# Second and third token group: the second expert product in seven block products, from split weights kept in DRAM

## The chip, the cores and the metric

The kernel runs on one core of a Trainium2 chip. The metric is the device time of one execution in microseconds (us). A core has TensorE (PE: matrix products into the PSUM banks), VectorE (DVE), ScalarE (ACT) and GpSimd (POOL) for elementwise work, SyncE (SP), which here only issues transfers, and 16 DMA engines between DRAM and the on-chip SBUF.

## The reference

An attention layer makes the 2304 x 512 input `x` of a mixture of experts; only the second half matters here:

```python
N, D, E, F = (2304, 512, 8, 1024)
P = ...                       # 2304 x 8, eight rounds of row and column scaling
for e in range(E):
    h = np.maximum(x @ w1[e], 0.0)
    ye = h @ w2[e]
    out += P[:, e:e + 1] * ye
```

All of it is float32, and all P are positive.

## The kernel before

Every float32 operand of a matrix product is held as two rounded parts, a high one (`h` at the end of a name) and a low one (`l`), and a product is three: high by high, high by low, low by high. ACT makes the high part (a copy), POOL or DVE the low part (a subtraction).

The experts come behind attention, in `experts()`. The 2304 tokens are three groups of 768. The work on one group, for one expert and one quarter (256 columns) of its hidden layer, is an **item**; a group has 31 of them (the 32nd, of expert 0, is done for all tokens during attention), and the groups follow each other, so that all weights are loaded and split three times over. An item has two products:

- The first, `x @ w1`, is 2 x 2 blocks by 2 x 2 blocks. `first_fast` makes it in seven block products instead of eight (a scheme of Strassen's kind): POOL makes four sums of weight blocks (L979 to L984), and `t_tasks` four sums of token blocks once for a group; a block product is six matmuls of 128x384 (L1024). DVE adds the products to the four quarters of h (L1055); ACT takes relu and the high part (L1008), DVE the low part (L1009). The items in the set `plain` (four at the start, two at the end of the first and of the second group) use eight block products.
- The second, `h @ w2`, is `product2`: 36 matmuls of 128x512 (L838), six for each 128 tokens, with h as the weights. DVE multiplies each result by P and adds it to `acc` (L1095), which goes to `out` at the end of a group.

PE does the first product of item q, then the second product of item q - 1. Meanwhile POOL and ACT split the weights of the items that follow (L969 to L998). On ACT and DVE the order is as the code has it, on the others a scheduler sets it; every engine runs its instructions in order, and waits where a result or a buffer isn't there.

## Time and profile before

| | |
|---|---|
| median of 3 runs | 1727.99 us (1727.05 to 1728.17) |
| the profiled execution | 1727.62 us, of which the span from first to last instruction is 1725.8 us |
| busy share of the span | PE 99%, DVE 72%, POOL 67%, ACT 41% |
| granted clock of PE | 1.00 of full speed (2.4 GHz) |
| DMA | 135 MB, mean 78 GB/s |

A busy share says how long an engine had an instruction in work, not that it worked at its peak, and a mean over the span hides stages with different limits.

### The profile page before, as it was taken

How to read it: one execution, taken by the hardware profiler on the slowest of the kernel's cores; microseconds unless marked ns; L12 is line 12 of the kernel's file. 1: busy time of each engine (PE TensorE's matmuls, PEld its weight loads, DVE VectorE, ACT ScalarE, POOL GpSimd, SP SyncE). 2: the span in 40 equal slices, each digit the busy share in tenths (PEclk: the TensorE clock that was granted, in tenths of full speed). 3: DMA queues.
4: the chain of work that ended last, by engine and by line, in shares of the span. 5: the costliest groups of instructions: out<-in, count | busy, mean ns of one | idle time of the engine just before them, and what ended most of it. 6: DMA issues, size and time to landing. Idle time of an engine off the chain costs nothing.

```text
span 1725.8 us, 26878 instructions
## 1 busy us (share of the span) xinstructions
PE 1707.8 (99%) x9381; PEld 1519.2 (88%) x9381; DVE 1250.3 (72%) x2307; ACT 707.1 (41%) x1632; POOL 1148.6 (67%) x1091
## 2 busy tenths in 40 slices
PE   7999999999999999999999999999999999999999
PEld 6777879899989999899989998899899998999887
DVE  8877747877777777777777777777777777777776
ACT  7877743333333333343333333332343333333332
POOL 5755544576667766577677666775677667766673
PEclk9999999999999999999999999999999999999999
DMA  5444333222222222232222222212332222212221
GB/s 137 101 108 103 94 110 107 68 61 62 74 74 68 61 68 74 74 129 68 73 74 62 61 74 74 71 60 73 93 116 60 68 73 74 63 60 73 74 62 49
DMA packets 150215, 135.02 MB, mean 78 GB/s; under 512 B 68288, under 2 KB 116544, under 8 KB 150080
## 3 DMA queue, kind: packets, MB, share of 16 engines
q1 hardware_dynamic: 148304, 132.22, 26.1%
q8 instruction: 74, 1.21, 0.3%
q10 hardware_dynamic: 1776, 1.09, 0.2%
q14 instruction: 61, 0.50, 0.1%
HBM read 123.75 MB, written 9.51 MB: 77 GB/s over the span
## 4 chain that ended last, share of the span: by engine, by line
PE 97%; DVE 1%; DMA 1%; ACT 1%; POOL 0%; issue 0%; SPq 0%; POOLq 0%; ACTq 0%; DVEq 0%
PE s L838 44%; PE s L1024 30%; PE f L1024 10%; PE x L648 2%; PE s L408 2%; PE s L489 1%; PE f L838 1%; PE f L817 1%; PE s L313 1%; PE s L455 1%; PE x L653 1%; PE s L623 1%; PE s L715 0%; PE s L540 0%; PE s L508 0%; PE s L817 0%
## 5 line engine op out<-in xcount | busy, mean ns | idle before, releaser
L975 POOL TENSOR_TENSOR w1l<-raw,w1h 128x512 fp32r<-128x512 f32 x263 | 365.9, 1404 | 396.0 <-ACT w1h L974 387.7
L1095 DVE SCALAR_TENSOR_TENSOR acc<-s,P,acc 128x512 f32<-128x512 f32 x540 | 395.0, 744 | 146.7 <-PE s L838 146.7
L838 PE MATMUL s<-w2h,hhl 128*128 128x512 f32 x1116 | 436.1, 391 | 0.0
L838 PE MATMUL s<-w2l,hhh 128*128 128x512 f32 x1116 | 435.8, 391 | 0.0
L838 PE MATMUL s<-w2h,hhh 128*128 128x512 f32 x1116 | 434.8, 390 | 0.0
L1055 DVE TENSOR_TENSOR temps<-s,temps 128x384 f32<-128x384 f32 x447 | 242.3, 554 | 173.2 <-ACT w1h L974 86.5
L1009 DVE SCALAR_TENSOR_TENSOR hhl<-temps,hhh 128x384 fp32r<-128x384 f32 x340 | 304.8, 896 | 0.0
L998 POOL TENSOR_TENSOR w2l<-raw,w2h 128x512 fp32r<-128x512 f32 x186 | 292.8, 1594 | 10.5 <-ACT w2h L997 10.5
L1008 ACT ACTIVATE hhh<-temps 128x384 fp32r<-128x384 f32 x340 | 178.7, 526 | 295.3 <-DVE temps L1055 287.7
L838 PEld LDWEIGHTS s<-w2h,hhl 128*128 128x128 f32 x1116 | 209.4, 188 | 43.9
L838 PEld LDWEIGHTS s<-w2h,hhh 128*128 128x128 f32 x1116 | 209.6, 188 | 42.4 <-DVE acc L1095 1.1
L838 PEld LDWEIGHTS s<-w2l,hhh 128*128 128x128 f32 x1116 | 209.5, 188 | 41.6
L1058 ACT COPY temps<-s 128x384 f32<-128x384 f32 x64 | 30.7, 480 | 416.2 <-PE s L1024 409.4
L1024 PE MATMUL s<-th,w1h 128*128 128x384 f32 x510 | 170.3, 334 | 0.0
L1024 PE MATMUL s<-tl,w1h 128*128 128x384 f32 x510 | 170.3, 334 | 0.0
L1024 PE MATMUL s<-th,w1l 128*128 128x384 f32 x510 | 170.3, 334 | 0.0
L1024 PE MATMUL s<-xh,w1l 128*128 128x384 f32 x480 | 161.3, 336 | 0.4 <-POOL w1l L970 0.4
L1024 PE MATMUL s<-xh,w1h 128*128 128x384 f32 x480 | 161.4, 336 | 0.0
L1024 PE MATMUL s<-xl,w1h 128*128 128x384 f32 x480 | 160.8, 335 | 0.0
L974 ACT CAST w1h<-raw 128x512 fp32r<-128x512 f32 x263 | 154.2, 616 | 3.0 <-DMA raw<-in_moe_w_dram 3.0
L1055 DVE TENSOR_TENSOR temps<-f,temps 128x384 f32<-128x384 f32 x148 | 80.3, 554 | 57.5 <-ACT w1h L974 28.5
L997 ACT CAST w2h<-raw 128x512 fp32r<-128x512 f32 x186 | 111.9, 607 | 0.0
(216 smaller groups left out, 2841.1 us busy)
## 6 DMA issues: line engine op xcount, KB each, us to landing
raw<-in_moe_w_dram SPq DMA_DIRECT2D x372, 256.0 KB
rsb<-rd SPq DMA_DIRECT2D x32, 144.0 KB
ydr<-wst SPq DMA_DIRECT2D x18, 256.0 KB
acc<-ydr SPq DMA_DIRECT2D x18, 256.0 KB
qraw<-in_q_dram SPq DMA_DIRECT2D x32, 128.0 KB
vraw<-in_v_dram SPq DMA_DIRECT2D x32, 128.0 KB
kraw<-in_k_dram SPq DMA_DIRECT2D x30, 128.0 KB
out_dram<-acc SPq DMA_DIRECT2D x15, 256.0 KB
```

Of the source, the lines that this page charges most:

```text
L408: nc.tensor.matmul(out=sp[h][:, at:at + w], lhsT=qq[x][half[h], 128 * i:128 * i + 128], rhs=kk[y][half[h], 0:w], start=(a == 0), stop=(a = ...
L648: nc.tensor.matmul(out=x[half[h], a0:a1], lhsT=vs[:, kt, h], rhs=ee(h), start=(kt == 0), stop=False,)
L838: nc.tensor.matmul(out=pt, lhsT=h_[:, f, cols], rhs=w[:, f], start=(n == 0), stop=(n == 5))
L974: nc.scalar.copy(out=wh[:, i:i + 2], in_=src)
L975: tt(out=wl[:, i:i + 2], in0=src, in1=f32(wh[:, i:i + 2]), op=ALU.subtract)
L997: nc.scalar.copy(out=wh[:, j], in_=raws[j])
L998: nc.gpsimd.tensor_tensor(out=wl[:, j], in0=raws[j], in1=f32(wh[:, j]), op=ALU.subtract)
L1008: nc.scalar.activation(out=hh[:, f, c], in_=src, func=AF.Relu)
L1009: late.append(lambda: nc.vector.scalar_tensor_tensor(out=hl[:, f, c], in0=src, scalar=0.0, in1=f32(hh[:, f, c]), op0=ALU.max, op1=ALU.subt ...
L1024: nc.tensor.matmul(out=pt[:, 0:HT], lhsT=w[:, wi, k], rhs=x[:, k], start=(n == 0), stop=(n == total - 1),)
L1055: nc.vector.tensor_tensor(out=o, in0=x, in1=y, op=ALU.add)
L1095: nc.vector.scalar_tensor_tensor(out=acc[:, j], in0=pt, scalar=P[:, t_, e:e + 1], in1=acc[:, j], op0=ALU.mult, op1=ALU.add,)
```

## The change

The first group stays, and writes its split weights to DRAM on the way: `keep` the seven parts of w1 with their low parts into `cache`, `keep2` three of the four blocks of w2 into `cache3`; `w1_again` makes those of the four plain items at the start. P goes to DRAM transposed (`pd`).

The second and third group are written as a list of timed steps (`at`), sorted by time (with a table `SHIFT` of some 700 numbers added, and a table `ON` that says whether DVE or POOL takes an operation), and all engines run in this order. Items go in pairs: both first products (`fast`), then both second products (`sums`). The second product is now transposed, with w2 as the weights and h (already multiplied by P, `pb`) as the moving side, and is also made in seven block products, two row halves each, with three matmuls of 128x384 for every half: 42 for an item. The two items of a pair add up in PSUM, and DVE adds the banks to 14 blocks `macc` (tiles `m`); two of the seven products stay in PSUM for the next pair. For the seven products, DVE and POOL make four sums of blocks of h (`combos`) and their low parts, and in the second group four sums of blocks of w2, which `cache2` keeps for the third. At the end of a group `group_end` joins `macc` to four quarters, and `close` turns them back by PE transposes, adds the start values from `ydr` and writes `out`. The last pair of the second group uses eight block products for the first product (`slow`), while `t_again` makes the token sums of the third group.

```diff
         ITEMS = [
-            (g, e, part) for g in range(NG) for e in range(E) for part in range(NQ)
-            if (e, part) != (0, 0)
+            (0, e, part) for e in range(E) for part in range(NQ) if (e, part) != (0, 0)
         ]
...
-        scaled = [(0, 1, 0)] + [(g, 0, 1) for g in range(1, NG)]
-        plain = set(range(4)) | {g * per - j for g in range(1, NG) for j in (1, 2)}
+        scaled = [(0, 1, 0)]
+        plain = set(range(4)) | {per - 1, per - 2}
+        cache = dram.tile([per, 8, 128, 2, 256], F32, name="cache")
+        cache2 = dram.tile([per, 2, 128, 512], F32, name="cache2")
+        cache3 = dram.tile([per, 3, 128, 2, 256], F32, name="cache3")
...
+            def keep(q=q, ops=slice(0, 7), to=slice(0, 7)):
+                for i, w in enumerate((wh, wl)):
+                    nc.sync.dma_start(
+                        out=cache[q, to, :, i].rearrange("o p c -> p o c"),
+                        in_=f32(w[:, ops]).rearrange("p o k c -> p o (k c)"),
+                    )
...
+            return [lambda: two(1, r1), lambda: one(0, a11)] + rest
...
-            return [lambda: one(0), lambda: one(1)]
+            def keep2():
+                for i, w in enumerate((wh, wl)):
+                    w = f32(w)
+                    nc.sync.dma_start(out=cache3[q, 0, :, i], in_=w[:, 0, 0:256])
+                    nc.sync.dma_start(
+                        out=cache3[q, 1:3, :, i].rearrange("o p c -> p o c"),
+                        in_=w[:, 1].rearrange("p (o c) -> p o c", o=2),
+                    )
+
+            return [lambda: one(0), lambda: one(1), keep2]
...
-        def second(q, j):
+        def second_mm(q, j):
+            product2(
+                py[j % 3], *hs[q % 2], *w2s[(q + 1) % 2], slice(128 * j, 128 * j + 128)
+            )
...
+        sb = py + [ps.tile([128, 512], F32, tag="x", name="sx", bufs=1)]
+        fb = pp
...
+        hop = [{n: (xs[0][i], xs[1][i]) for i, n in enumerate(HB)}, {}]
+        wr = [x for a in range(2) for x in cut(w1s[1][a], 512)] + cut(w1s[0][0], 512)[0:1]
...
+        def who(key):
+            return (dv, po)[ON.get(kind[0] + key, ON[key])]
...
+        def w1_get(q, op, t):
+
+            i = ring["n"] % len(wr)
+            ring["n"] += 1
+            at(ring["free"][i] + 0.1, lambda: sy.dma_start(
+                out=f32(wr[i]), in_=cache[q, op].rearrange("p a c -> p (a c)")
+            ), "wl")
+            ring["free"][i] = t + U
...
+        def halves(t, j, n, src):
+
+            at(t, lambda: ac.copy(out=hop[j][n][0], in_=src), f"{n}H{j}")
+            at(t + 0.6, tt(who(f"{n}L{j}"), hpart(j, n, 1), src, hpart(j, n, 0, True),
+                           ALU.subtract), f"{n}L{j}")
...
+        def quarter(t, j, n, src):
+
+            dst = FQS[n]
+            at(t, lambda: dv.scalar_tensor_tensor(
+                out=dst, in0=src, scalar=0.0, in1=pb[int(n[2]) - 1], op0=ALU.max, op1=ALU.mult
+            ), f"{n}F{j}")
+            if n != "b12":
+                halves(t + 0.55, j, n, dst)
...
+            for n, d, o, x, y in (
+                ("t1", 6.4, f1, f12, f11), ("t3", 7.95, f12, f22, f12), ("t2", 8.9, f2, f22, f1),
+                ("t4", 9.95, f21, f21, f2),
+            ):
+                at(t + d, tt(who(f"{n}S{j}"), o, x, y, ALU.subtract), f"{n}S{j}")
+                halves(t + d + 1.0, j, n, o)
...
+        def fast(t, g, q, j):
...
+            for k, (op, x) in enumerate(plan):
+                w, b = w1_get(q, op, t + k * U), next_bank()
+                at(t + k * U, lambda w=w, x=x, b=b: mm1(b, w, x, True, True), "", 6)
...
+            A = ALU.add
+            at(t + 1.15, lambda: ac.copy(out=X, in_=p1), f"X{j}")
+            at(t + 2.2, tt(dv, f11, p2, X, A), f"c11{j}")
+            quarter(t + 2.65, j, "b11", f11)
+            at(t + 3.25, tt(dv, U2, p6, X, A), f"U2{j}")
+            at(t + 4.3, tt(dv, V, p5, U2, A), f"V{j}")
+            at(t + 5.3, tt(dv, f12, p3, V, A), f"c12{j}")
+            quarter(t + 5.8, j, "b12", f12)
+            at(t + 6.4, tt(dv, U2, p7, U2, A), f"U3{j}")
+            at(t + 6.85, tt(dv, f22, p7, V, A), f"c22{j}")
+            quarter(t + 7.3, j, "b22", f22)
+            at(t + 7.75, tt(dv, f21, p4, U2, A), f"c21{j}")
+            quarter(t + 8.2, j, "b21", f21)
+            combos(t, j)
+            return t + 7 * U
...
+        def sums(t, js, order, spread, done, hold):
...
+            parts = [(n, a, j) for n, a in blocks_ for j in js]
+            if len(js) == 2:
+                head = [p for p in parts if p[0] in order[:4]]
+                parts = sorted(head, key=lambda p: p[2]) + parts[len(head):]
...
+            def mm(n, a, j):
+                wn, hn = USE[n]
+                w, x = wop[wn][j], hop[j][hn]
+                for i, (p, r) in enumerate(((0, 0), (1, 0), (0, 1))):
+                    pe.matmul(
+                        out=bank[n, a][:, 0:HT], lhsT=w[p][:, 128 * a:128 * a + 128], rhs=x[r],
+                        start=(j == js[0] and i == 0 and (n, a) not in held),
+                        stop=(j == js[-1] and i == 2 and not (hold and n in order[5:])),
+                    )
...
+                    at(t1, tt(dv, m, b, m, ALU.add), f"E{n}{a}")
...
+        def w2_ops(g, q, e, part, j, start, order, step):
...
+                from_ = cache2[q, i] if again else w2[e, r0:r0 + 128, :]
+                at(rfree[j] + 0.05 * i, lambda i=i, from_=from_: sy.dma_start(
+                    out=raw[j][i], in_=from_
+                ), f"w2l{j}")
...
+            if not again:
+                for i, n in enumerate(("s1", "s3", "s2", "s4")):
+                    key = f"{n}S{j}"
+                    at(t0 + 2.0 * i + j, tt(who(key), *sums_[n]), key)
...
+                if n in sums_:
+                    t = max(t, t0 + (0.0 if again else 8.0 + j))
+                    src = sums_[n][0]
+                    at(t, lambda n=n, src=src: ac.copy(out=wop[n][j][0], in_=src()), f"{n}H{j}")
+                    at(t + 0.5, tt(po, lambda n=n: wop[n][j][1], src,
+                                   lambda n=n: f32(wop[n][j][0]), ALU.subtract), f"{n}L{j}")
...
+                else:
+                    k = ("a11", "a12", "a22").index(n)
+                    at(wfree[n] + 0.1, lambda n=n, k=k: sy.dma_start(
+                        out=f32(kept[n][j]), in_=cache3[q, k].rearrange("p a c -> p (a c)")
+                    ), f"w2k{j}")
...
+            if not again:
+                for i in range(2):
+                    at(t0 + 8.5 + j, lambda i=i: sy.dma_start(out=cache2[q, i], in_=raw[j][i]),
+                       f"w2s{j}")
...
+            def turn(c):
+                b, o = bk[c]
+                for a in range(2):
+                    pe.transpose(
+                        b[:, o + 128 * a:o + 128 * a + 128],
+                        macc[SUM[i, th], a][:, 128 * c:128 * c + 128], ident,
+                    )
...
+            def add(c):
+                b, o = bk[c]
+                y, t_ = stage(g, n)[:, c], 6 * g + 3 * th + c
+                dv.scalar_tensor_tensor(
+                    out=y, in0=y, scalar=P[:, t_, 0:1], in1=b[:, o:o + 256],
+                    op0=ALU.mult, op1=ALU.add,
+                )
+                eng = (sy, ac)[c % 2] if g == NG - 1 else sy
+                eng.dma_start(
+                    out=out[128 * t_:128 * t_ + 128, 256 * i:256 * i + 256], in_=y
+                )
...
+        for g in range(1, NG):
+            us = [[(0, 1)]] + [[(0, 2), (0, 3)]] + [
+                [(e, 2 * i), (e, 2 * i + 1)] for e in range(1, E) for i in range(2)
+            ]
+            s_prev = now - 8.0
+            for u, items in enumerate(us):
...
+                order = LAST if last_u else ODD if u % 2 else EVEN
...
+                t0 = now
+                for j in js:
+                    q = 4 * items[j][0] + items[j][1] - 1
+                    now = (slow if last_u and g < NG - 1 else fast)(now, g, q, j)
...
+                    for n in range(4):
+                        close(now, g - 1, n, bk[2 * n:2 * n + 2], now + 0.4)
...
+                    if g < NG - 1:
+                        t_again(t0 - 13.5, g + 1)
...
+                now = sums(now, js, order, group_end(g) if last_u else {}, wfree, not last_u)
...
+        seq.sort(key=lambda x: x[:2])
+        with tc.manual_schedule():
+            for x in seq:
+                x[2]()
```

Where the instructions stand. PE, middle of the second group, the change from one product to the other. Before (`w2h`, `w2l`, `hhh`, `hhl`: high and low part of w2 and h):

```order
L838 MATMUL s<-w2h_74,hhh_3909 128x512
L838 MATMUL s<-w2l_75,hhh_3909 128x512
L838 MATMUL s<-w2h_74,hhl_3910 128x512
L1024 MATMUL s<-xh,w1h_3903 128x384
L1024 MATMUL s<-xl,w1h_3903 128x384
L1024 MATMUL s<-xh,w1l_3904 128x384
```

And now (blocks of h lie in freed parts of `xh`, `xl` and in `hb`, weights in freed parts of the old tiles `w1h` to `w2l` and in `wu`):

```order
L1567 MATMUL s<-tl,w1h_3902 128x384
L1567 MATMUL s<-th,w1h_3902 128x384
L1688 MATMUL s<-xh,w2h_74 128x384 x2
L1688 MATMUL s<-xl,w2h_74 128x384
L1688 MATMUL s<-xh,w2h_74 128x384 x2
L1688 MATMUL s<-xl,w2h_74 128x384
L1688 MATMUL s<-xh,w2l_75 128x384 x2
```

The matmuls of 512 columns are gone; three of 384 fill a block, and 84 of them follow each other for a pair.

DVE, same place. Before, one item:

```order
L1055 TENSOR_TENSOR temps<-f,temps 128x384
L1055 TENSOR_TENSOR temps<-s,temps 128x384 x2
L1009 SCALAR_TENSOR_TENSOR hhl_3908<-temps,hhh_3907 128x384
L1055 TENSOR_TENSOR temps<-s,temps 128x384
L1055 TENSOR_TENSOR temps<-f,temps 128x384 x2
L1009 SCALAR_TENSOR_TENSOR hhl_3908<-temps,hhh_3907 128x384
L1055 TENSOR_TENSOR temps<-s,temps 128x384
L1009 SCALAR_TENSOR_TENSOR hhl_3908<-temps,hhh_3907 128x384
L1095 SCALAR_TENSOR_TENSOR acc<-s,P,acc 128x512
L1009 SCALAR_TENSOR_TENSOR hhl_3908<-temps,hhh_3907 128x384
L1095 SCALAR_TENSOR_TENSOR acc<-s,P,acc 128x512 x5
```

And now, behind the last first product of a pair (`raw`, `f_8325`, `temps` hold quarters of h and their sums; `s` and `f` are PSUM banks):

```order
L1595 SCALAR_TENSOR_TENSOR temps<-temps,pb 128x384
L1595 SCALAR_TENSOR_TENSOR raw<-raw,pb 128x384
L1595 SCALAR_TENSOR_TENSOR temps<-temps,pb 128x384
L1546 TENSOR_TENSOR raw<-raw,temps 128x384
L1546 TENSOR_TENSOR hb<-temps,hb 128x384
L1546 TENSOR_TENSOR f_8325<-temps,raw 128x384
L1546 TENSOR_TENSOR hb<-raw,hb 128x384
L1546 TENSOR_TENSOR raw<-temps,raw 128x384
L1546 TENSOR_TENSOR hb<-f_8325,hb 128x384
L1546 TENSOR_TENSOR temps<-temps,f_8325 128x384
L1546 TENSOR_TENSOR m<-s,m 128x384 x2
```

Before, no two instructions in a row of an item had both inputs in SBUF; now ten such follow each other.

## Rows read from the trace of the kernel before

**Rows 1.** The page: busy time of each engine, and the chain by engine.

```profile
PE 1707.8 (99%) x9381; PEld 1519.2 (88%) x9381; DVE 1250.3 (72%) x2307; ACT 707.1 (41%) x1632; POOL 1148.6 (67%) x1091
...
PE 97%; DVE 1%; DMA 1%; ACT 1%; POOL 0%; issue 0%; SPq 0%; POOLq 0%; ACTq 0%; DVEq 0%
```

**Rows 2.** Busy time by stretch, two items in the second group.

```profile
core 0: us, PE busy (x) PEld busy (x) DVE busy (x) ACT busy (x) POOL busy (x), PEclk, DMA share, GB/s
900.00:931.04 31.04, 31.04 (x158) 28.15 (x157) 22.46 (x35) 10.92 (x22) 22.24 (x22) 1.00 0.23 69
```

**Rows 3.** Timeline of PE: start us, us, instruction; from first to second product and back.

```profile
1237.81 0.33 PE L1024 MATMUL f<-th,w1h 128*128 128x384 f32 x1
...
1239.89 0.39 PE L838 MATMUL s<-w2h,hhh 128*128 128x512 f32 x1
...
1248.09 0.33 PE L1024 MATMUL s<-xh,w1h 128*128 128x384 f32 x1
```

**Rows 4.** Timeline of DVE: one item of the second group, start of the next.

```profile
907.01 0.56 DVE L1055 TENSOR_TENSOR temps<-s,temps 128x384 f32<-128x384 f32 x1 [1.42 <-ACT w1h L974]
...
909.50 0.63 DVE L1009 SCALAR_TENSOR_TENSOR hhl<-temps,hhh 128x384 fp32r<-128x384 f32 x1
...
911.10 1.02 DVE L1055 TENSOR_TENSOR temps<-s,temps 128x384 f32<-128x384 f32 x2 [0.31 <-PE s L1024]
...
913.17 1.19 DVE L1009 SCALAR_TENSOR_TENSOR hhl<-temps,hhh 128x384 fp32r<-128x384 f32 x1
...
914.95 1.00 DVE L1009 SCALAR_TENSOR_TENSOR hhl<-temps,hhh 128x384 fp32r<-128x384 f32 x1
...
922.52 0.56 DVE L1055 TENSOR_TENSOR temps<-s,temps 128x384 f32<-128x384 f32 x1 [1.42 <-ACT w1h L974]
```

**Rows 5.** Timeline of POOL: the same item.

```profile
908.97 0.74 POOL L979 TENSOR_TENSOR raw<-raw 128x256 f32<-128x256 f32 x1
909.79 0.94 POOL L980 TENSOR_TENSOR raw<-raw 128x256 f32<-128x256 f32 x1
...
912.32 3.20 POOL L998 TENSOR_TENSOR w2l<-raw,w2h 128x512 fp32r<-128x512 f32 x2
```

**Rows 6.** Groups: busy us, mean ns of one, then idle time before them.

```profile
L1095 DVE SCALAR_TENSOR_TENSOR acc<-s,P,acc 128x512 f32<-128x512 f32 x540 | 395.0, 744 | 146.7 <-PE s L838 146.7
...
L1009 DVE SCALAR_TENSOR_TENSOR hhl<-temps,hhh 128x384 fp32r<-128x384 f32 x340 | 304.8, 896 | 0.0
...
L1055 DVE TENSOR_TENSOR temps<-s,temps 128x384 f32<-128x384 f32 x447 | 242.3, 554 | 173.2 <-ACT w1h L974 86.5 <-PE s L1024 78.6 <-ACT w2h L997 1.4
...
L489 PE MATMUL s<-ident,e 128*128 128x128 f32 x224 | 30.2, 273 | 0.0
```

**Rows 7.** Single lines: duration ns min/median/max.

```profile
L1009 DVE SCALAR_TENSOR_TENSOR hhl<-temps,hhh x340: 545/880/1759, 333.5 to 1707.3; 128x384 fp32r<-128x384 f32 x170
...
L975 POOL TENSOR_TENSOR w1l<-raw,w1h x263: 1274/1306/2037, 251.9 to 1694.7; 128x512 fp32r<-128x512 f32 x132
...
L984 POOL TENSOR_TENSOR raw<-raw x85: 735/741/745, 318.4 to 1689.3; 128x256 f32<-128x256 f32 x85
```

**Rows 8.** Transfers: busy by stretch (last: DMA share, GB/s), then issues on SP.

```profile
1249.00:1254.00 5.00, 5.00 (x30) 5.00 (x29) 2.58 (x6) 1.83 (x4) 3.49 (x4) 1.00 1.06 398
...
921.50:928.00 6.50, 6.50 (x39) 6.41 (x38) 4.20 (x8) 3.10 (x7) 5.22 (x7) 1.00 0.00 1
...
917.13 1.62 SPq L947 DMA_DIRECT2D raw<-in_moe_w_dram  x2
```

**Rows 9.** Timeline: the end of the program.

```profile
1721.22 0.39 PE L838 MATMUL s<-w2h,hhl 128*128 128x512 f32 x1
1721.65 0.75 DVE L1095 SCALAR_TENSOR_TENSOR acc<-s,P,acc 128x512 f32<-128x512 f32 x1 [0.61 <-PE s L838]
1722.43 0.34 ACTq L1101 DMA_DIRECT2D out_dram<-acc  x1
```

More of the change, by code (lines that the diff above doesn't have):

```diff
@@ L1098, in second @@
                 )
[L1099 to L1101 removed]
+            if q == per - 1:
+                nc.sync.dma_start(out=out[128 * t_:128 * t_ + 128, :], in_=acc[:, j])
+        def second(q, j):
+            second_mm(q, j)
+            second_add(q, j)
         def acc_scale(g, j):
@@ new lines, in mm1, with blocks @@
+        def mm1(bank, w, x, first, last):
+            n = 0
+            for k in range(2):
+                for a, b in ((0, 0), (0, 1), (1, 0)):
+                    pe.matmul(
+                        out=bank[:, 0:HT], lhsT=w[:, a, k], rhs=x[b][:, k],
+                        start=bool(first and n == 0), stop=bool(last and n == 5),
+                    )
+                    n += 1
+        def blocks(g):
+            bs = {
+                (k, t): (blk(xh, g, k, t), blk(xl, g, k, t)) for k in range(2) for t in range(2)
+            }
+            ts = [
+                tuple(t_[:, i].rearrange("p (k c) -> p k c", k=2) for t_ in tcomb)
+                for i in range(4)
+            ]
+            return bs, ts
@@ L1182 @@
+        kind[0] = "2l:"
+        for n in range(4):
+            t = now + (-6.0, -2.0, -0.6, 0.75)[n]
+            close(t, NG - 1, n, fb[2 * (n % 2):2 * (n % 2) + 2], t + 0.4)
+        seq.sort(key=lambda x: x[:2])
+        with tc.manual_schedule():
+            for x in seq:
+                x[2]()
     setup()
```

389 lines of the change are left out of this document (356 added, 33 removed), and 192 rows, old and new, of tables (ON, SHIFT).

## The prediction, made before the changed kernel ran

> **What bounds the kernel now.** I read the page first: PE is busy for 99% of the span and holds 97% of the chain that ended last [rows 1], so a gain has to come out of PE's own instructions. The busy time by stretch says how much room the others have in the groups that change: in 31.04 us, two items, PE has no gap, DVE is busy for 22.46 us, POOL for 22.24, ACT for 10.92, DMA for 0.23 of its time [rows 2]. The timeline of PE gives the price of a matmul by the distance of starts, since the printed durations overlap: the 12 matmuls of 384 columns from 1237.81 to 1239.89 are 0.1733 us apart, the 36 of 512 from 1239.89 to 1248.09 are 0.2278 [rows 3]. An item is thus 42 x 0.1733 + 36 x 0.2278 = 7.28 + 8.20 = 15.48 us, and two starts of an item, 907.01 and 922.52, are 15.51 apart [rows 4]. PE sets the pace, at the full clock [rows 2].
>
> The second thing to see is what DVE and POOL do to each other. DVE's instructions that read PSUM take 554 ns at any time [rows 6], but L1009 with both inputs in SBUF takes from 545 ns up to 1759, 896 in the mean [rows 6, 7]. The two timelines side by side show why. POOL's L979 runs until 909.71, and the L1009 that started at 909.50 ends at 910.13; L980, started at 909.79, then takes 0.94 instead of some 0.74. The first of two L998 ends half way, at 913.92, and the L1009 of 913.17 ends at 914.36; the second ends at 915.52, and that of 914.95 at 915.95 [rows 4, 5]. Every time L1009 ends 0.42 to 0.44 us behind POOL's instruction: a DVE instruction with two inputs in SBUF and a POOL instruction don't run together, and the later one waits for the whole of the other. I call the former S instructions, and those that read PSUM P instructions.
>
> **The change, part by part.** The sum is made against the profiled execution, 1727.6 us (span 1725.8); the median of the runs shown, 1728.0, is 0.4 above it.
>
> *PE, items.* 42 matmuls of 384 columns take the place of 36 of 512: 7.28 for 8.20 us, so that an item is 14.56 instead of 15.48 (15.51 as it ran). For the 62 items of the two groups: 62 x 0.95 = 58.9 us less. The four items in eight block products stay four.
>
> *PE, turning back.* 48 transposes of 128x128, at 30.2 us for 224 of them [rows 6], 0.135 each: +6.5. The end of the program: now one DVE instruction and a transfer stand behind the last matmul [rows 9]; then two additions of 0.47, six transposes (counted) and three DVE instructions of about 0.4: +2.
>
> Floor with PE never waiting: 1727.6 - 58.9 + 6.5 + 2 = **1677.2**.
>
> *DVE in a pair of the second group.* The program has, between pairs, 24 P instructions of 384 columns and on average 25.5 S of 384 and 3.5 S of 256. A P and a free S cost 0.47 back to back (two in 1.02 less the overlap [rows 4]); S of 256 I set at 0.33. Own work: 11.3 + 12.0 + 1.2 = 24.5 us, where PE needs 29.12. In the third group 24 P and 23.5 S: 22.3.
>
> *The waits between DVE and POOL.* For an S instruction L1009 gives both ends: 0 where POOL is idle (minimum 545) and 0.35 in the mean (896 - 545), where POOL worked through the whole stretch, with instructions of 1.05 us in the mean (0.74 for 256 columns, 1.3 for 512, 1.6 when it waits itself [rows 5, 7]). In the new pair POOL has 12.5 instructions of 256 columns and 4.5 of 384 (1.02 between the two rows), 13.8 us plus waits of its own, some 55% of 29.12, and 0.81 us each: 0.35 x 0.81/1.05 x 0.55 = 0.15 us for an S instruction. In the third group 8 and 6.5, some 48%, 0.87: 0.14. I take 0.15 for both. Second group: 24.5 + 29 x 0.15 = 28.9 us of DVE for 29.12 of PE: full. An engine that is full, runs in order and sometimes has to wait for PE holds PE back a little; I take 0.4 for each of the 13 plain pairs: +5. Third group: 22.3 + 3.5 = 25.8, room enough; 0.2 for each of 15 pairs: +3.
>
> *The end of the second group.* Its last two pairs and the single item behind them carry the token sums, the joining of the blocks and the 12 additions of `close`: by the program 28.8 + 31.1 + 14.2 = 74 us of own DVE work with 90 S instructions, so 87.6 with waits; PE has 29.1 + 31.2 (four block products more) + 17.8 = 78.1. Before, the same sums were spread over DVE's free time. +9.
>
> *The start of the second group.* `macc` lies where `acc` was, and can't be written before the six transfers to `out` are done; the last second product of the first group and the first single item lie in between. 0 to 6 us, I take 2.
>
> *Transfers.* A pair loads 14 x 256 KB of w1 parts, 6 of w2 parts, 4 of w2, and writes 4 back: 7.5 MB in 29.12 us, 258 GB/s against 69 before. The trace has 398 GB/s over 5 us (DMA share 1.06) at a change of groups [rows 8], so this is some two thirds of what was reached. The seven buffers of the w1 parts leave 6 x 1.04 = 6.2 us from a buffer's last read to its next use; four transfers issued by 918.4 were gone by 921.5 (1 GB/s afterwards) [rows 8]. SP issues some 29 times 0.4 us in 29 us. I cost it at nothing, covered by PE's work on the other six buffers; without that cover each of 14 loads would cost its 2 to 3 us, 30 us for a pair.
>
> *First group.* The stores of `keep` stand behind POOL's last split on SP, where the next loads wait for the same instruction and are needed an item later: nothing; 28 instructions of POOL and 16 of DVE for `w1_again` go into 4.4 us of free POOL time for each item [rows 2]: nothing.
>
> Sum: 1677.2 + 5 + 3 + 9 + 2 = **1696**.
>
> **The rivals.**
>
> *All hidden.* The order was made so that POOL's instructions fall under DVE's P instructions; with waits near 0, DVE has 24.5 of 29.1 us and only the end of the group costs something: 1677 to 1688. For it: in the third group DVE has 6.8 us of room. Against it: ten S instructions in a row in the listing, where POOL can only come in between. 22%.
>
> *Most of it eaten.* Waits of 0.17 to 0.22 for an S instruction: at 0.20 the second group's pair is 24.5 + 5.8 = 30.3, and 0.4 for the waits on PE, 1.6 x 13 = 21; the end 74 + 18 - 78 = 14; start 2 to 6; third group 0.4 x 15 = 6: 1677 + 21 + 14 + 4 + 6 = 1722. 21%, of which 6% within 0.2% of before.
>
> *Slower.* POOL has a waiting instruction at the end of every S instruction of a run, and comes in each time. The gain is gone where the mean wait passes 0.235 us: 13 x (24.5 + 6.8 + 0.4 - 29.1) = 34, end 17, third group 3, start 2, in sum 56 for 50. At the 0.35 of L1009 the second group's pair is 34.7 us, 13 x 5.6 = 72, the end 27, the third group 22.3 + 8.2 = 30.5, 15 x 1.4 = 21, together 1677 + 122 = 1799. For it: L1009 has that mean now. Against it: POOL's instructions are shorter and fewer. 15%.
>
> The Trainium skill (SBUF — State Buffer, "Who interferes with whom") states the rule behind this rival: a DVE instruction with two SBUF inputs contends with a GpSimd instruction that reads SBUF, and the one that starts second fully blocks until the other is done. Our trace agrees, with the 0.42 to 0.44 us above; by the rule taken to its end, each of the 17 POOL instructions of a pair stops DVE for its full length, 24.5 + 13.8 = 38.3 us, and the second group alone would lose 13 x 9.2 = 120 us.
>
> *Weights come late.* SP runs in order, and a load that waits for a buffer of w2 holds the w1 loads behind it. One product waiting 1 us in each pair is +30 us: 1726. It is in the two cases above with a few per cent.
>
> **How the numbers follow.** Forecast 1688 to 1706: 42%; all hidden 22% (4% of it below 1674); eaten 21%; slower 15%. The likeliest gives 1696. A measurement of this kernel can tell about 0.2%, 3.4 us: faster than 1724.5 has 42 + 22 + 15 = 79%, the same 6%, slower 15%. The range takes in the first three: 1674 to 1730. It leaves out 4% below and some 16% above.
>
> **What the changed profile would show.** PE's matmuls of 384 columns still 0.173 apart, and an item of 14.6 us of PE work in the third group. If the forecast holds, pairs are 29.1 to 29.5 us in the third group and 29.3 to 30 in the second, PE's idle time there ended by DVE (a bank not yet read, or an `hb`, `xl` part not there), and the longest idle time around the last pair of the second group. S instructions have a mean near 0.70 us. If they stand at 0.8 or more, it is one of the two costly rivals; if PE's idle time ends with a transfer into a `w1` part, the weights are late. I would be wrong downwards if the order keeps POOL clear of DVE's runs, and upwards if PE loses full speed in gaps, for which the rows before (clock 1.00 everywhere) have no price.

## The result and the profile after

The changed kernel takes 1740.85 us (median of 4 runs, 1737.17 to 1742.61), the kernel before 1728.08 beside it: a ratio of 1.0072, 95% interval 1.0054 to 1.0089. It is slower by 0.7%, where 1696 was forecast; it lies outside the range, on the side to which I gave 15%. The profiled execution took 1740.03 us, its span 1738.2.

The page of the changed kernel, answering to [rows 1]: busy time by engine, and the chain.

```profile
PE 1687.8 (97%) x9803; PEld 1556.7 (90%) x9803; DVE 1400.4 (81%) x2884; ACT 695.7 (40%) x1736; POOL 968.2 (56%) x1020
...
PE 74%; DVE 17%; DMA 4%; issue 2%; ACT 1%; POOL 1%; SPq 0%; DVEq 0%; ACTq 0%; POOLq 0%
```

PE held 97% of the chain; now it is 74, and DVE's share has gone from 1 to 17%. PE waits for others, and the question is where. The busy time by stretch (columns as in [rows 2]) cuts the second and third group into the start, the plain pairs, the change of groups, the plain pairs of the third group and the last pair; then come one even and one odd pair of the third group:

```profile
751.30:848.40 97.10, 87.62 (x458) 83.11 (x457) 73.00 (x136) 30.67 (x72) 48.34 (x56) 0.95 0.81 265
848.40:1179.20 330.80, 328.20 (x1849) 319.34 (x1849) 295.55 (x584) 113.04 (x264) 169.69 (x185) 1.00 0.77 253
1179.20:1267.80 88.60, 82.33 (x458) 78.45 (x458) 81.67 (x161) 28.89 (x68) 41.23 (x42) 0.98 0.63 208
1267.80:1695.40 427.60, 416.66 (x2353) 405.89 (x2352) 356.95 (x663) 142.31 (x343) 186.99 (x206) 1.00 0.66 214
1695.40:1738.20 42.80, 34.29 (x194) 31.22 (x192) 37.17 (x75) 8.07 (x18) 14.71 (x15) 0.98 0.47 154
1420.60:1450.80 30.20, 29.59 (x169) 29.02 (x169) 24.96 (x47) 10.35 (x26) 14.57 (x17) 1.00 0.59 192
1450.80:1481.40 30.60, 29.83 (x169) 28.92 (x169) 25.79 (x48) 9.59 (x23) 11.83 (x13) 1.00 0.74 237
```

The gap between length and PE's busy time names the places, but understates them: a printed matmul ends some 0.16 us behind the next one's start, and one at half the clock counts as busy. So I take the distance of each two starts less the price of the first, 0.1733 us for 384 columns and 0.2278 for 512 [rows 3], and 0.109 for a transpose, and call the rest a **stop**. From the begin of the second group (751.3) they add up to 64.5 us, by place:

| place | forecast | stops after | stops in the fastest version (below) |
|---|---|---|---|
| start: single item and two pairs | 2.8 | 16.1 | 4.9 |
| 11 further plain pairs of the second group | 4.4 | 10.6 | 2.1 |
| its last two pairs and the change of groups | 9 | 11.0 | 5.4 |
| 14 pairs of the third group | 2.8 | 20.1 | 3.4 |
| last pair and end of the program | 0.2 | 6.7 | 5.6 |

(0.4 was forecast for each of 13 pairs of the second group, two of which stand in the first line, and 0.2 for each of 15 of the third, the last of them in the last line.) Without its stops the changed kernel would take 1740.0 - 64.5 = 1675.5 us. (The fastest version has one stop more, of 1.8 us, just ahead of its second group, which the table leaves out.)

**An even pair of the third group.** The timeline of DVE, from the pair that begins at 1359.6:

```profile
1361.92 0.56 DVE L1546 TENSOR_TENSOR temps<-s,temps 128x384 f32<-128x384 f32 x1 [3.90 <-PE s L1567]
1362.51 1.06 DVE L1595 SCALAR_TENSOR_TENSOR temps<-temps,pb 128x384 f32<-128x384 f32 x1
...
1364.62 1.10 DVE L1546 TENSOR_TENSOR xl<-temps,xh 128x384 fp32r<-128x384 f32 x1
...
1370.95 0.95 DVE L1546 TENSOR_TENSOR temps<-temps,f 128x384 f32<-128x384 f32 x1
...
1372.96 1.22 DVE L1595 SCALAR_TENSOR_TENSOR temps<-temps,pb 128x384 f32<-128x384 f32 x1
...
1376.90 1.21 DVE L1546 TENSOR_TENSOR temps<-s,temps 128x384 f32<-128x384 f32 x2
```

Those of POOL and of PE, same pair:

```profile
1361.72 1.43 POOL L1546 TENSOR_TENSOR w1l<-rawb,w1h 128x256 fp32r<-128x256 f32 x2 [0.51 <-ACT w1h L1745]
```

```profile
1376.56 0.34 PE L1688 MATMUL s<-xl,w1h 128*128 128x384 f32 x1
1377.50 0.61 PE L1688 MATMUL s<-xh,w1h 128*128 128x384 f32 x2 [0.61 <-DVE temps L1546]
```

DVE waits 3.90 us for the pair's first product, and then has no gap above 0.12 us up to the bank read of 1376.90, for which PE stops (1377.50 less 1376.56 less 0.17: 0.77 us). In that stretch four of its instructions wait for POOL, like the one of 1362.51, which ends 0.42 us behind POOL's `w1l`: 0.50 + 0.54 + 0.39 + 0.66 = 2.1 us more than the 0.56 of a free one. PE pays 0.8 of these 2.1 us. DVE is busy for 24.96 of 30.20 us in such a pair; the idle time comes first, then the waits, then the read.

**An odd pair** stops twice: 0.34 us for a bank read, and at the second item's first product. PE and SP, pair of 1511.6:

```profile
1530.75 0.34 PE L1688 MATMUL f<-xl,w2h 128*128 128x384 f32 x1
1532.39 1.30 PE L1688 MATMUL s<-hb,w1l 128*128 128x384 f32 x6 [1.31 <-ACT hb L1588]
```

```profile
1526.94 0.32 SPq L1751 DMA_DIRECT2D w1l<-cache  x1
```

The view names ACT's `hb` as the releaser here, the transfer into `w1l` in other pairs. It is the transfer in all five pairs with this stop: what lies in that old tile now is a kept block of w2, and by the trace's semaphore updates its load lands 0.13 to 0.14 us ahead of PE's start each time (here at 1532.26). The load was issued 5.4 us before PE could start.

**The start.** PE and SP; then the window of the full queues, and the one behind the stop:

```profile
757.52 0.34 PE L1567 MATMUL s<-th,w1l 128*128 128x384 f32 x1
761.38 0.69 PE L1567 MATMUL f<-th,w1h 128*128 128x384 f32 x1 [3.52 <-DMA w1h<-cache]
```

```profile
751.30 0.41 SPq L1037 DMA_DIRECT2D cache<-w1l  x1
758.19 0.33 SPq L1557 DMA_DIRECT2D w1h<-cache  x1
```

```profile
752.00:758.00 6.00, 5.86 (x34) 5.54 (x32) 2.11 (x6) 0.48 (x1) 1.07 (x2) 1.00 1.06 373
761.40:764.80 3.40, 3.40 (x10) 3.11 (x11) 0.00 (x0) 0.22 (x1) 1.80 (x3) 0.50 0.75 61
```

SP has issued the last store of `keep` at 751.30 and stands with the seventh load until 758.19: its buffer, in `w1h`, is still read by the store that was issued ahead of that one, at 750.60. Everything behind it waits too. The chain of what ended last begins with that store and follows the queue on through three more transfers:

```profile
750.60 7.53 DMA cache<-w1h
...
759.05 7.92 DMA pb<-pd
...
767.03 5.31 DMA cache<-raw
...
795.02 5.21 DMA w2h<-cache
```

### The profile page after: what moved, and what is told of

The parts are those of the page before. It is cut to its first block, busy times and chain, and to the rows that moved or that the text cites. A ratio compares the mean times of both kernels' runs of the same rounds, so it can differ in the third digit from the quotient of the medians.

```text
span 1738.2 us, 29930 instructions
## 1 busy us (share of the span) xinstructions
PE 1687.8 (97%) x9803; PEld 1556.7 (90%) x9803; DVE 1400.4 (81%) x2884; ACT 695.7 (40%) x1736; POOL 968.2 (56%) x1020
## 4 chain that ended last, share of the span: by engine, by line
PE 74%; DVE 17%; DMA 4%; issue 2%; ACT 1%; POOL 1%; SPq 0%; DVEq 0%; ACTq 0%; POOLq 0%
PE s L1688 15%; PE s L854 14%; PE s L1567 11%; PE s L1100 10%; DVE temps L1546 5%; PE f L1567 4%; PE f L1100 3%; PE sx L1688 3%; PE x L648 2%; DVE raw L1546 2%; DVE temps L1595 2%; PE s L408 2%; DVE xl L1546 2%; DVE m L1546 1%; PE s L489 1%
## 5 line engine op out<-in xcount | busy, mean ns | idle before, releaser
L1032 POOL TENSOR_TENSOR w1l<-raw,w1h 128x512 fp32r<-128x512 f32 x85 | 117.3, 1393 | 117.0 <-ACT w1h L1031 83.0
L1174 DVE SCALAR_TENSOR_TENSOR acc<-s,P,acc 128x512 f32<-128x512 f32 x168 | 123.0, 744 | 37.5 <-PE s L854 37.0
L854 PE MATMUL s<-w2h,hhh 128*128 128x512 f32 x372 | 147.0, 395 | 0.7 <-DVE acc L1174 0.7
L854 PE MATMUL s<-w2h,hhl 128*128 128x512 f32 x372 | 146.1, 393 | 0.0
L854 PE MATMUL s<-w2l,hhh 128*128 128x512 f32 x372 | 146.1, 393 | 0.0
L1065 POOL TENSOR_TENSOR w2l<-raw,w2h 128x512 fp32r<-128x512 f32 x62 | 98.0, 1598 | 2.0 <-ACT w2h L1064 2.0
L854 PEld LDWEIGHTS s<-w2h,hhh 128*128 128x128 f32 x372 | 70.4, 189 | 17.8 <-DVE acc L1174 4.3
L854 PEld LDWEIGHTS s<-w2h,hhl 128*128 128x128 f32 x372 | 70.2, 189 | 15.0
L854 PEld LDWEIGHTS s<-w2l,hhh 128*128 128x128 f32 x372 | 70.3, 189 | 13.6
L1085 DVE SCALAR_TENSOR_TENSOR hhl<-temps,hhh 128x384 fp32r<-128x384 f32 x100 | 81.0, 810 | 0.0
```

Source lines behind the costliest of these rows:

```text
L854: nc.tensor.matmul(out=pt, lhsT=h_[:, f, cols], rhs=w[:, f], start=(n == 0), stop=(n == 5))
L1032: tt(out=wl[:, i:i + 2], in0=src, in1=f32(wh[:, i:i + 2]), op=ALU.subtract)
L1065: nc.gpsimd.tensor_tensor(out=wl[:, j], in0=raws[j], in1=f32(wh[:, j]), op=ALU.subtract)
L1085: late.append(lambda: nc.vector.scalar_tensor_tensor(out=hl[:, f, c], in0=src, scalar=0.0, in1=f32(hh[:, f, c]), op0=ALU.max, op1=ALU.subt ...
L1174: nc.vector.scalar_tensor_tensor(out=acc[:, j], in0=pt, scalar=P[:, t_, e:e + 1], in1=acc[:, j], op0=ALU.mult, op1=ALU.add,)
```

## The experiments

Each kernel differs from the changed one, and each ratio is to the kernel before. I had two theories. **Place:** what stops PE is which DVE instruction a lock wait falls ahead of, and when a load is issued. **Amount:** DVE, or the DMA engines, have too much to do.

**Less work for DVE and POOL.** The first kernel leaves out POOL's low parts of the w2 sums in plain pairs (but the first of each), the second DVE's low parts of the h sums in the third group, so that PE multiplies old data there.

```diff
-                    at(t + 0.5, tt(po, lambda n=n: wop[n][j][1], src,
...
+                    if (n, j) not in lows or kind[0] not in ("k:", "m:", "n:", "o:"):
+                        lows.add((n, j))
+                        at(t + 0.5, tt(po, lambda n=n: wop[n][j][1], src,
...
```
```diff
         def halves(t, j, n, src):
...
+            if kind[0] in ("n:", "o:") and n[0] == "t" and who(f"{n}L{j}") is dv:
+                return
```

> Left out: POOL's eight low parts of w2 block sums in each plain pair (from the third pair of the second group on; the product takes stale ones). POOL loses 8 x 0.74 = 5.9 us of 12 to 19 a pair. If the waits between DVE and POOL set PE's stops: mean of the DVE instructions with two SBUF inputs falls from 0.58-0.60 to about 0.56 in the second group and from 0.64 to about 0.58 in the third; DVE gains 1 to 1.5 us a pair, the stops of 1.1 us in the even pairs of the third group go to 0.3 or less, those of the odd pairs (1.5 to 2.2) to under 1; 1740.9 - 13 x 0.6 - 13 x 0.8 = about 1723. Rival, the stops come from late weights and from the written order, not from lost DVE time: the mean falls likewise, but the stops stay within 0.3 of what they were, 1737 to 1741.

Measured: 1736.10 us, 1.0044 (1.0029 to 1.0059). Even pairs of the third group stop 0.51 instead of 1.07 us, odd ones still 0.8 to 2.2, and the even pairs of the second group 1.2 to 1.7. The result lies outside both of the stated bounds, nearer to the rival.

> Left out: in the plain pairs of the third group those low parts of the sums t1 to t4 that DVE makes, four in an even pair, six in an odd one (1.9 and 2.8 us of DVE back to back). If DVE's own load between the first products and the start of the sums is what stops PE: even pairs from 1.1 us of stop to under 0.3, odd pairs from 1.5-2.2 to under 0.5, pairs of 29.1 to 29.5 us, in sum 7 x 0.9 + 7 x 1.4 = 16, 1725. Rival, weights late in the odd pairs: only the even pairs and the first 0.34 us of the odd ones gain, the second stop of the odd pairs (0.75 to 1.5, at the first product of the second item) stays or grows; 6 + 2 = 8 less, 1733. Rival, nothing but the order counts: no change.

Measured: 1736.34 us, 1.0043 (1.0026 to 1.0060). Even pairs stop mostly 0.25 us, odd pairs 0.5 to 2.0 with one of 4.13, where the second item's first product waits for the load of `w1l`. So taking work off bought 4 to 5 us of 64, and the odd pairs have another cause beside it.

**No loads.** Plain pairs of the third group compute with old weights.

```diff
-            at(ring["free"][i] + 0.1, lambda: sy.dma_start(
+            if kind[0] not in ("n:", "o:"):
+                at(ring["free"][i] + 0.1, lambda: sy.dma_start(
...
-                    at(wfree[n] + 0.1, lambda n=n, k=k: sy.dma_start(
+                    if kind[0] not in ("n:", "o:"):
+                        at(wfree[n] + 0.1, lambda n=n, k=k: sy.dma_start(
```

> Left out: all loads of w1 parts and of the three kept w2 blocks in the plain pairs of the third group (the products take what the buffers hold). If late weights make the second stop of the odd pairs: those go from 1.5-2.2 us to 0.3-0.5, the even pairs stay at 1.1; 7 x 1.3 = 9 less, 1732. If transfers cost nothing, as I had predicted: every pair as it was, 1740.

Measured: 1738.65 us, 1.0061 (1.0046 to 1.0076). Odd pairs stop 1.50 us, all alike, even ones 1.07 as before, and the longest stop at the change of groups goes from 4.59 to 2.70. Taking these loads away gains 2 us, no more; the sum of bytes is not the bound.

**The start, two versions.** The seventh load goes to another buffer, in the second version early.

```diff
-        ring = dict(n=0, free=[-9.0] * (len(wr) - 1) + [-5.0])
+        ring = dict(free=[-9.0] * (len(wr) - 1) + [9.0])
...
-            i = ring["n"] % len(wr)
-            ring["n"] += 1
+            i = min(range(len(wr)), key=lambda i: ring["free"][i])
```

> The whole computation; the seventh load of a w1 part of the second group goes into the first buffer again instead of the one whose store of the first group is still running. If SP standing 6.2 us on that buffer is what stopped PE for 3.7 us and lowered its clock for 3.4 us: both go, 3.7 + 2.7 us less, 1734.5. Rival, the DMA engines are full there with the last stores (377 GB/s) and the loads land no earlier: under 1.5 us less.

Measured: 1747.16 us, 1.0111 (1.0096 to 1.0126). Missed: the load now stood on SP behind those of P and w2, was issued at 761.76, and PE stopped for 10.9 us.

```diff
-            at(ring["free"][i] + 0.1, lambda: sy.dma_start(
+            at(-3.0 if ring["free"][i] == U else ring["free"][i] + 0.1, lambda: sy.dma_start(
```

> The whole computation. As e3, but the seventh load stands ahead of the loads of P and of the kept w2 blocks on SP, behind which it had been caught in e3 (issued at 761.8 instead of 758.2). If only its place on SP was wrong: it is issued near 753, lands behind the last stores of the first group (1.8 MB at 375 GB/s, until about 757.5), PE doesn't stop at 757.7 and keeps its clock: 3.7 + 2.7 less, 1734.5. Rival, the DMA engines are full from 745 on and the load lands at 760 all the same: 1 us less.

Measured: 1746.12 us, 1.0106 (1.0091 to 1.0121). Here, and in the two kernels that follow next, the new order let some instructions take other data than they should (here the load stood ahead of the first product that still reads the buffer, which then waited 10.4 us for it), so that these three times test neither theory.

**Bank reads ahead of low parts**, alone and with the other edits.

```diff
-            "k:t4L1": 2.004, ... "n:t4L0": 3.049, ... "o:U31": 3.186, ... "o:c211": 2.044, ... "o:t1L0": 7.192, ... "o:t4L0": 4.205,
+            "k:t4L1": 1.5, ... "n:t4L0": 4.45, ... "o:U31": 1.15, ... "o:c211": -0.08, ... "o:t1L0": 9.3, ... "o:t4L0": 6.0,
```

> The whole computation. On DVE alone the order changes: in the even pairs of the third group the two reads that free the last two banks stand ahead of four other instructions, in its odd pairs one low part that is needed late goes behind such a read, in the even pairs of the second group a low part of t4 goes ahead of one addition. If it is the written order that is bad: the even pairs of the third group from 1.07 to about 0.3, the first stop of the odd ones (0.34) and the one of 0.45 in the even pairs of the second group gone: 7 x 0.75 + 7 x 0.3 + 6 x 0.4 = 10 less, 1731. Rival, DVE has more work there than fits, in whatever order: the stop moves to another place, and the time stays within 2 us of 1741.

> The whole computation; e5, e6 and e7 together. If all three causes are of the order: 1740.9 - 6.4 - 6.5 - 10 = 1718, under the kernel before. If DVE's load and the transfers bound those stretches: 1735 or more.

Measured: 1747.07 us, 1.0109 (1.0092 to 1.0126), and 1744.88 us, 1.0100 (1.0085 to 1.0115).

**Kept weights loaded earlier**, in odd pairs of both groups.

```diff
-            "m:w2k0": 14.134, ... "n:w2k1": 16.039,
+            "m:w2k0": 8.0, ... "n:w2k1": 8.0,
```

> The whole computation. The loads of the kept w2 blocks, of the first item in the odd pairs of the second group and of the second item in the odd pairs of the third, stand 6 to 8 us earlier in the written order. If their place in the order makes them late: the stop of 2.6 us in front of the first sums of pair 1 goes with its 1.5 us of lowered clock, the 0.2 to 0.3 in front of the sums of the other odd pairs go too (5 x 0.25), and the odd pairs of the third group fall from 1.8 to the 1.5 they had without loads (7 x 0.3 = 2): 1734. Rival, the transfers come in a bunch and fill the DMA engines (380 to 400 GB/s where they are late), so that another load is late instead: within 1.5 us of 1741.

Measured: 1737.23 us, 1.0052 (1.0037 to 1.0067). The first pair stops 1.09 instead of 4.31 us, odd pairs of the third group 1.5 each.

**Another order for everything.** All numbers of `SHIFT` and `ON` are set anew, so that bank reads come before lock waits and loads earlier; `ON` may choose the engine for each item and pair kind, which moves 4 to 10 operations of a pair between DVE and POOL. The computation, its operations and its transfers stay whole. The second and third kernel do this for the pairs of one group alone.

```diff
-            return (dv, po)[ON.get(kind[0] + key, ON[key])]
+            return (dv, po)[next(ON[k] for k in (kind[0] + key, key, key[:-1], key[:-2]) if k in ON)]
...
-                    at(t + 0.5, tt(po, lambda n=n: wop[n][j][1], src,
+                    at(t + 0.5, tt(who(f"{n}L{j}"), lambda n=n: wop[n][j][1], src,
```

> The whole computation, with the same instructions: only the table of times (SHIFT) and the table of who takes a sum or low part (ON) are others, in both groups; in a plain pair 4 to 10 operations change between DVE and POOL. If the loss is one of order (work of DVE standing ahead of a result or a bank that PE needs next, loads standing late on SP): plain pairs fall to 29.1 to 29.3 us, so 10.6 - 2 less in the second group and 20 - 3 less in the third, about 5 less at each change of groups, 2 at the end: 1741 - 9 - 17 - 10 - 2 = 1703, between 1690 and 1710. Rival, DVE's load bounds the pair (own work 24.5 us with 3 to 5 us in which no product is ready, and the waits for POOL): no order helps, pairs stay at 29.6 to 30.5, 1735 or more.

Measured: 1706.94 us, 0.9877 (0.9862 to 0.9892); stops 28.0 us.

> The whole computation; the other tables for the third group alone. If order is the cause there: its pairs at 29.1 to 29.3 instead of 30.2 and 30.6 to 31.3, 17 less, and 2 less at the end of the program: 1722. Rival (DVE's load bounds the third group): 1738 or more.

Measured: 1723.56 us, 0.9976 (0.9966 to 0.9986); third-group pairs stop 0.01 to 0.5 us, one of them 1.5.

> The whole computation; the other tables for the plain pairs of the second group alone. If order is the cause there: pairs at 29.1 to 29.3 instead of 29.6 and 30.4, 9 less, and some 3 more in the first two pairs: 1729 to 1732. Rival (in this group DVE is full, 24.5 us of own work and the waits): within 3 us of 1741.

Measured: 1729.92 us, 1.0014 (1.0004 to 1.0023); second-group pairs 0.03 to 0.34, two of them 0.6 and 0.7. With the same operations, another order and another sharing out between DVE and POOL are worth 34 us; no run has the one without the other.

**The start again, whole.** The loads of P and the seventh load go ahead of the last stores of `keep`, the seventh into buffer 0, and the first w2 loads and splits into buffers still being stored move back; once with the new order, once with the old. (With the old one the two numbers of the last lines are 0.15 and 1.5, and the splits stay where they were.)

```diff
-            i = ring["n"] % len(wr)
+            n = ring["n"]
+            i = n % 6 if n < 7 else (1, 2, 3, 4, 5, 0, 6)[n % 7]
...
-            at(ring["free"][i] + 0.1, lambda: sy.dma_start(
+            at(ring["free"][i] + (3.3 if n == 6 else 0.1), lambda: sy.dma_start(
...
-            at(-6.0, f, "held", 2)
+            at(4.4, f, "held", 2)
```

> The whole computation; f1_all_order with another start of the second group: P and the seventh w1 load go to SP ahead of the two stores (1.8 MB) that keep the split weights of the first group's last item, the seventh load into the first buffer again once the first product has read it, and the splitting of w2 into the stored buffers later. If the stops at the start come from these stores (the seventh load waited 6.8 us for them on SP, and pb behind it, landing 9 us after issue): the 1.1 and 4.6 us in unit 0 and the clock lost behind them go, 5 to 6 less, 1701. Rival, the transfers of the start fill the DMA engines in any order and another load is late: within 2 us of 1707.

Measured: 1700.63 us, 0.9843 (0.9827 to 0.9860), the fastest version here; stops 21.4 us. Its busy time by stretch: the plain pairs of the second group, the pairs of the third, then an even and an odd pair of the third:

```profile
840.50:1163.00 322.50, 322.50 (x1851) 320.03 (x1850) 282.85 (x569) 114.86 (x265) 182.25 (x205) 1.00 0.78 260
1245.90:1656.90 411.00, 410.20 (x2354) 407.51 (x2354) 354.87 (x691) 147.41 (x342) 173.80 (x177) 1.00 0.68 223
1393.20:1422.60 29.40, 29.40 (x170) 29.10 (x170) 26.90 (x51) 11.20 (x26) 13.88 (x15) 1.00 0.60 197
1422.60:1451.70 29.10, 29.10 (x169) 29.10 (x169) 24.10 (x49) 9.63 (x22) 10.77 (x11) 1.00 0.76 249
```

And DVE in the even pair that begins at 1334.7:

```profile
1337.76 0.55 DVE L1572 TENSOR_TENSOR temps<-s,temps 128x384 f32<-128x384 f32 x1
...
1347.43 0.76 DVE L1622 SCALAR_TENSOR_TENSOR temps<-temps,pb 128x384 f32<-128x384 f32 x1
...
1350.10 1.21 DVE L1572 TENSOR_TENSOR temps<-s,temps 128x384 f32<-128x384 f32 x2
...
1354.96 1.18 DVE L1572 TENSOR_TENSOR hb<-temps,hb 128x384 fp32r<-128x384 f32 x1
```

In the third group this speaks for place and against amount: DVE has 691 instructions instead of 663, in an even pair 26.90 us in 51 against 24.96 in 47, and still the bank read comes 15.4 us after the pair's begin instead of 17.3. DVE begins 0.75 us later, but between the pair's first product and the read stand 23 instructions instead of 26, and one short wait (0.2 us) instead of four. The others fall behind the read, as at 1354.96, where PE waits for nobody. Nor is it that POOL has less to do: it has 13 us less in this group, and the kernel without POOL's low parts, where it has 84 us less (102.65 us), loses 6 us of this group's stops, this one 17. In the second group the sharing went the other way (DVE 569 instructions instead of 584, 12.7 us less; POOL 205 instead of 185), so that there place and amount aren't told apart.

> The whole computation; the changed kernel with the same change at the start. If the stores are the cause: the 3.7 us stop and the 2.7 us of lowered clock behind it go, 1734. Rival: the time lost moves to the loads behind (pair 1's stop of 2.6 us grows), 1739 or more.

Measured: 1741.63 us, 1.0081 (1.0065 to 1.0096). With the old order PE's first stop fell from 3.7 to 1.9 us, but the one at `acc` in the first group's last second product went from 0.85 to 2.5, and that of the first pair, for a w2 load, from 2.6 to 3.0. The start is 2 us better (14.1 for 16.1), the whole no faster. That the time lost goes on to the next load in the queue fits this, but isn't shown: the two versions differ in the splits of w2 and in the numbers too.

**Odd pairs of the third group: two causes or one?** First the order alone (three operations change engine, twelve numbers of `SHIFT`), then with the load 8 us earlier.

```diff
-"n:t1L0": 1, ... "n:t4L0": 0,
+"n:t1L0": 0, ... "n:t4L0": 1, "n:b11L0": 1,
...
-            "n:U21": -0.446, ... "n:b11L0": 0.833, ... "n:c111": 1.242, ... "n:t4H1": 2.522,
+            "n:U21": 0.97, ... "n:b11L0": 4.55, ... "n:c111": 0.87, ... "n:t4H1": 1.88,
```

> The whole computation; only the odd pairs of the third group change: two low parts that are needed late (b11 and t4 of the first item) go from DVE to POOL, one that is needed early (t1 of the first item) from POOL to DVE, and twelve operations move by 0.4 to 3.7 us in the table. DVE has one instruction less, 47 for 48. If the place of the work decides: those pairs from 1.5-2.2 us of stop to under 0.3, 7 x 1.5 = 11 less, 1730, the even ones as they were (1.07). Rival, the amount of DVE's work decides: one instruction of some 0.5 us less, and in e2 six fewer took 0.5 from a pair, so at most 0.3 a pair, 1739.

Measured: 1740.12 us, 1.0067 (1.0051 to 1.0084). Neither: the bank read's stop is gone, but the pairs still stop 0.5 to 1.8 us (one 3.8), nearly all of it at the second item's first product and now plainly for the load, which lands 0.13 to 0.14 us ahead of PE's start in all six pairs with this stop. PE in the pair of 1570.6:

```profile
1589.13 0.34 PE L1688 MATMUL f<-xl,w2h 128*128 128x384 f32 x1
1591.43 0.94 PE L1688 MATMUL s<-hb,w1l 128*128 128x384 f32 x3 [1.96 <-DMA w1l<-cache]
```

```diff
-            "n:w2k1": 16.039,
+            "n:w2k1": 8.0,
```

> The order of the odd third-group pairs of e9_odd_small, and with it the load of the kept weights of the second item issued 8 us earlier in these pairs; the computation is whole. If the stops of the odd pairs have two causes side by side, the place of DVE's instructions and a load that is issued late, each of which covers the other: both are gone, the odd third-group pairs stop 0.3 us or less instead of 1.5 to 2.2, and the time is 1726 to 1732 us (1740.9 less 8 pairs x 1.4). If a third cause stands behind them (a queue that is full, so that the earlier load lands no earlier), the odd pairs keep 0.7 us and more, and the time is 1735 or more.

Measured: 1731.65 us (11 runs, 1726.96 to 1736.10), 1.0017 (1.0008 to 1.0026). The pair of 1512.4, by its busy time:

```profile
1512.40:1541.50 29.10, 29.10 (x170) 29.10 (x169) 23.70 (x47) 9.79 (x23) 12.96 (x14) 1.00 0.76 249
```

The kept block lands 6.4 us ahead of its matmul there. Five of seven odd pairs stop 0.01 us (the pair of 1452.8 stops 0.3, the one of 1274.5 at the group's begin 0.42). Two causes lay side by side: removing the late load alone left 1.5 us a pair, the order alone 0.5 to 3.8, both together next to nothing, and 9.2 us less in all (1740.85 to 1731.65).

## Why the prediction was wrong

**The floor was right.** 1677.2 was forecast for a PE that never waits, 1675.5 came out, though the first group took 1.8 us more (below); 42 matmuls of 384 columns at 0.1733 us are an item, as reckoned. The error is in the stops, 64.5 us for a forecast of 19. By the table the plain pairs of both groups cost 23.5 us more than forecast, the start 13.3, the two ends 8.5.

**The waits between DVE and POOL: their size was too high, and their place was left out.** The groups of DVE's S instructions in the third group, 1298.4 to 1695.4 (columns as in [rows 6]; `f` is the tile `f_8325` here):

```profile
L1595 DVE SCALAR_TENSOR_TENSOR temps<-temps,pb 128x384 f32<-128x384 f32 x78 | 55.7, 735 | 0.5
...
L1546 DVE TENSOR_TENSOR raw<-temps,raw 128x384 f32<-128x384 f32 x26 | 19.3, 744 | 0.2
L1546 DVE TENSOR_TENSOR temps<-temps,f 128x384 f32<-128x384 f32 x20 | 18.7, 933 | 0.0
...
L1546 DVE TENSOR_TENSOR f<-temps,raw 128x384 f32<-128x384 f32 x26 | 14.4, 554 | 0.0
```

Over all groups of 384 columns the mean is 0.65 us here (305 instructions, 198.7 us) and 0.61 in the second group's plain pairs (279, 169.9): waits of 0.10 and 0.06 us beside a free one of 0.55, where I had 0.14 and 0.15. S instructions thus stand below the 0.70 that the forecast named, and by the sum of my prediction the time should have come out lower. But I compared two sums over a pair: 25.8 us of DVE for 29.12 of PE, "room enough", at 0.2 us a pair. The room is real and lies in the wrong place: 3.9 us in one piece at the begin, where DVE waits for the first product. From there to the bank read it has none, and 2.1 us of waits in between cost PE 0.8. 14 pairs cost 20.1 us instead of 2.8, the odd ones among them in part for a late load. The second group, forecast as full, cost 10.6 instead of 4.4; there too I had taken a mean over a pair, but whether DVE's order or its amount stops PE there stays open. The rule that the Trainium skill gives (SBUF — State Buffer, "Who interferes with whom") held for the four waits above (0.41 to 0.42 us behind the end of POOL's instruction); taken to its end, as the prediction did, it would have cost 13.8 us a pair of the second group, where the groups give 25.4 x 0.06 = 1.5.

**Transfers, "cost at nothing": the other step that failed.** I compared 258 GB/s with 398, two means again. At the start the queues were full (DMA share 1.06 at 373 GB/s), a store of 7.5 us held a buffer, and SP runs in order; later a single load issued 5 to 6 us ahead of its reader was too late. The stops at 761.38, 800.27 and 1259.02, each for a transfer or for work behind one, and the lowered clock after them are 16.7 us. At the change of groups the longest stop, 4.59 us, also begins with a transfer. The chain of the changed kernel there, and DVE:

```profile
1249.25 7.32 DMA m<-ydr
...
1257.46 0.56 DVE raw L1546
...
1258.05 0.99 ACT xh L1588 x2
```

```profile
1256.67 0.48 DVE L1807 SCALAR_TENSOR_TENSOR m<-m,P,sx 128x256 f32<-128x256 f32 x1 [2.13 <-DMA m<-ydr]
```

An addition of `close` waits on DVE for its start values, and behind it stands the sum that PE needs. In this profile my 6.2 us of buffer held for the w1 parts but the seventh at the start; the kept weights, P and the start values, which have no such buffer, I hadn't priced.

**The start of the second group**, 0 to 6 us taken as 2, cost 16.1 with its two first pairs, and I had looked for it in `acc` and `macc` alone. **First group**, nothing: the same matmul that begins the second group starts at 751.32, before the change at 749.57, so the group cost 1.8 us, in seven steps of some 0.3; no run took them apart. That its last stores would still run then, and what they hold up, stands under this point too. **The end of the second group**, 9, was 11.0. **The end of the program**: 2 us lay in the floor, 6.7 came on top, in stops for `xl` (2.0) and for joined blocks (1.5 and smaller); no run took these apart.

**The clock** was named as a way to be wrong upwards, and it was one, by 5.8 of the 64.5 us (below).

**The rivals.** "Slower" came true, but not by its mechanism, which needed a mean wait past 0.235 us. "Weights come late" was the nearer one, at a few per cent and as a cost of each pair; its sign, idle time of PE that ends with a transfer, stands in the profile at 761.38, 800.27 and in the odd pairs. What I had no rival for is a sum that fits while its order doesn't. That the forecast's time can be had from these operations is shown by the fastest version: 1700.63 us.

**What stays open:** which of the loads at the start would have to move for the old order to gain; what stops PE in the second group's pairs; and the last pair's stops, 5.6 us in the fastest version too.

## What to carry to other kernels

An engine with room in the mean can still hold up another: follow, from its idle time on, what stands between that and the instruction that is waited for, and add up the waits there alone. Price each transfer by the time from its issue to its landing when the queues are full, and look for who stands behind it on an engine that runs in order. Where a wait has two causes, removing one can show little; try both together before you drop either.

## What the runs showed of the hardware that was not expected

After a long stop PE ran at half the clock, a price that I had called unknown. In the changed kernel idle times of PE of 3.52 us (before 761.38), 2.44 (800.27) and 4.43 (1259.02) each come with a stretch at the lower level, 1.2 GHz (0.50 from 761.40 to 764.80, in the window above); one of 1.86 us (1713.82) does not. The starts there lie 0.32 us apart for 384 columns instead of 0.173, and 0.43 for 512 instead of 0.228: from 761.86 to 764.74, eight matmuls, 1.3 us more. The lower level lasts until 767.1 there and costs 2.7 us, 1.6 and 1.5 in the other two places. After a shorter idle time the first matmul alone takes some 0.1 us more (two matmuls at 1377.50 print 0.61 us instead of 0.51).

Transfers in small pieces may take the DMA engines' time out of proportion; this is read from one window, no run tested it. In the version with the new order alone, P (`pb`, by the code in pieces of 128 numbers, 512 bytes) is issued at 759.64, and its first reader on DVE waits 5.17 us for it. The window and the reader:

```profile
760.00:766.00 6.00, 5.94 (x30) 5.32 (x31) 3.20 (x7) 0.72 (x3) 0.00 (x0) 1.00 0.73 140
```

```profile
768.51 0.56 DVE L1621 SCALAR_TENSOR_TENSOR raw<-raw,pb 128x384 f32<-128x384 f32 x1 [5.17 <-DMA pb<-pd]
```

The engines are busy for 0.73 of the time at 140 GB/s, where 0.76 gave 249 in the odd pair above. Other transfers lie in the window too.

The versions scatter differently: 11 runs of the last experiment lie within 9.1 us, the four of the fastest version within 0.6. Why, no run shows; the kernel with the odd pairs' order alone, whose PE waits for loads too, stays within 1.7.
